# Channels innermost, two additions swapped between VectorE and GpSimd, and new slots, in a kernel of one FFT convolution and one feed-forward block

## The chip, the cores and the metric

One core of a Trainium2 chip. The time is the device time of one execution in microseconds (us). The kernel before took 2484.07 us in the runs that the prediction had (2483.41 to 2486.37). TensorE is PE below, its weight loads PEld, VectorE DVE, ScalarE ACT, GpSimd POOL, SyncE SP. SBUF and PSUM are the two memories in which this kernel keeps its tiles; PE's products are written to tiles in PSUM. All runs in this document are in the fast state and gave correct results. Wherever two kernels are compared, a ratio is the mean time of one kernel's fast runs over that of the other's of the same rounds, on the same chip, so it is not quite the ratio of the medians that stand beside it; the interval after it is the 95% one. Differences of ratios are turned into time with 2481 us, about what the kernel before takes on the chips used.

## The reference

```python
# batch, seq, d = 4, 12544, 128;  d_ff = 768
h = (np.maximum(pos_emb @ w1, 0) @ w2) * np.exp(-0.01 * pos)[:, None]
u = x * v
L = 2 * S
y = irfft(rfft(u, L, axis=1) * rfft(h, L, axis=0)[None], L, axis=1)[:, :S]
a = (x * y).reshape(B * S, D)
hid = maximum(maximum(a @ w1, a @ w2), a @ w3)
out = hid @ w_out
```

Four batches, each a long convolution (by Fourier transforms written as products with tables), then a feed-forward block.

## The kernel before: the parts that matter

The span has four stages: a **prologue** (spectrum of the filter, first half of batch 0); a **loop** of 45 rounds, which makes the rest of batch 0's convolution with nothing beside it; its short **drain**; and the **feed-forward part**, in which PE runs through the blocks of one batch while the convolution of the next is dealt out into "slots", one slot after each `up` (the products pa and pb with their maximum hid, some 3.3 us). An instruction that waits holds up those that stand behind it on its engine: in the profile before, at 793.60 us, ACT begins a turn after 5.93 us of waiting for dt, the hid behind it follows at 794.24, and PE, which had waited 1.90 us for that hid, goes on at 794.79; 28 of PE's 30 waits for ACT's hid before pb end after such a turn.

The first halves land in PSUM and are combined into `spec` in SBUF, two channels (`s`) at a time. Here the innermost index of the write is `k`, so neighbouring elements lie 1024 bytes apart in `spec`:

```python
    def by_r(ps):
        return ps[:].rearrange("p (s m) -> p s m", m=256)[:, :, 0:2 * N1].rearrange(
            "p s (r k) -> p s r k", r=2)

    def over_w(ps, dst, tmp):
        v = by_r(ps)
        nc.scalar.copy(tmp, v[:, :, 1, :])
        for c, op in enumerate((ALU.add, ALU.subtract)):
            nc.vector.tensor_tensor(out=dst[:, :, c, :].rearrange("p k s -> p s k"), in0=tmp,
                                    in1=v[:, :, 0, :], op=op)
```

A group `g` (45 to a batch) is two frequencies: product with the spectrum (`second`, `swap`, `re`, `im`, `sum`), inverse product (`third`), and the sums over halves (`over_c`, `turn`, `pair`, `store`):

```python
    def g_im(g):        # xs *= ht : both inputs in SBUF
        nc.vector.tensor_tensor(out=xss[g][:], in0=xss[g][:], in1=hts.pop(g)[:, 1], op=ALU.mult)

    def g_sum(g):       # xt += xs : both inputs in SBUF ("pointwise sum")
        nc.gpsimd.tensor_tensor(out=xts[g][:], in0=xts[g][:], in1=xss.pop(g)[:], op=ALU.add)
    # ... g_third: PE product, ACT copies half of it out ...
    # g_over_c: dt = c0 +- c1 (DVE, one buffer);  g_turn: two copies of dt on ACT (turn by -i)
    def g_pair(g):      # zs = dt[0:2] +- dt[2:4] : both inputs in SBUF ("sums of k1")
        dt = zss[g]
        zs = state["cv"][0].tile([P, 2, 2, D], FP32, tag="z", name="zs", bufs=2)
        for a, op in enumerate((ALU.add, ALU.subtract)):
            nc.vector.tensor_tensor(out=zs[:, a], in0=dt[:, 0:2, :], in1=dt[:, 2:4, :], op=op)
        zss[g] = zs

    def g_store(b, g):
        nc.gpsimd.dma_start(zd[b][2 * g:2 * g + 2].rearrange("k c t f -> (c t) k f"), ...)
```

The slots in the feed-forward part (the second figure orders the steps within a slot), and the loop:

```python
        s0 = int((NU - done) * 0.6 * per_pair) + 13
        for g in range(NK):
            s = s0 + int(g * per_pair)
            # ... loads
            at(s, 1, g_second, g)
            at(s + 1, 0, g_swap, g)
            at(s + 1, 0, g_re, g)
            at(s + 2, 0, g_im, g)
            at(s + 3, 0, g_sum, g)
            at(s + 5, 1, g_third, g)
            at(s + 6, 0, g_over_c, g)
            at(s + 6, 1, g_turn, g)
            at(s + 7, 1, g_pair, g)
            at(s + 9, 0, g_store, b, g)
    # ...
    for s in range(-1, NK + 5):          # the loop
        # ... s_filter(s), g_second(s), g_swap(s), g_re(s)
        # ... g_turn(s - 3), g_third(s - 2), g_im(s), g_sum(s)
        if 0 <= s - 3 < NK:
            g_pair(s - 3)
        if 0 <= s - 2 < NK:
            g_over_c(s - 2)
        if 0 <= s - 4 < NK:
            g_store(0, s - 4)
```

On DVE and GpSimd there also stand, in every slot, work of the feed-forward block: DVE takes the maximum `hid` (its input pb from PSUM), GpSimd sums of `hid` tiles (SBUF to SBUF). Where a DVE instruction is called blocked below, this is meant: in the profile before, the product xs, both inputs in SBUF, takes 675 to 687 ns in the 106 cases without a two-input instruction of GpSimd beside it, and 1183 ns on average, at most 2315, in the 74 with one; hid, with its input pb from PSUM, takes 559 ns without and 561 with.

Of the kernel before, what the change touches and what calls it, by code (L numbers as in the profile page):

```python
# [9 lines left out]
FP32 = mybir.dt.float32  # L10
I32 = mybir.dt.int32
U16 = mybir.dt.uint16
ALU = mybir.AluOpType
ACTF = mybir.ActivationFunctionType
PSUM = bass.MemoryType.PSUM
P = 128
# [11 lines left out]
N1 = 90  # L28
# [47 lines left out]
def kernel(  # L76
# [15 lines left out]
    nc = tc.nc  # L92
# [5 lines left out]
    NK = N1 // 2  # L98
# [35 lines left out]
    def first_halves(ps, lhs, table):  # L134


        for i, a in enumerate(lhs):
            for r in range(2):
                for c in range(2):
                    nc.tensor.matmul(  # L140
                        ps[64 * c:64 * c + 64, 256 * i + r * N1:256 * i + (r + 1) * N1],
                        a[:, r, :], table[:, r, c * N1:(c + 1) * N1],
                        start=(i % 2 == 0 and r == 0), stop=True, skip_group_check=True)

    def by_r(ps):
        return ps[:].rearrange("p (s m) -> p s m", m=256)[:, :, 0:2 * N1].rearrange(
            "p s (r k) -> p s r k", r=2)

    def over_w(ps, dst, tmp):

        v = by_r(ps)
        nc.scalar.copy(tmp, v[:, :, 1, :])  # L152
        for c, op in enumerate((ALU.add, ALU.subtract)):
            nc.vector.tensor_tensor(out=dst[:, :, c, :].rearrange("p k s -> p s k"), in0=tmp,  # L154
                                    in1=v[:, :, 0, :], op=op)

    def as_it_is(ps, dst):
        nc.scalar.copy(dst.rearrange("p k r s -> p s r k"), by_r(ps))

    def pair_mm(ps, w, x):  # L160

# [72 lines left out]
    sml = fin.enter_context(tc.tile_pool(name="sml", bufs=1))  # L234
# [81 lines left out]
    NU = NG  # L316
# [4 lines left out]
    us, uts, ws, hts, xts, xss, pss, zss = ({} for _ in range(8))  # L321
# [63 lines left out]
    def u_first(u, h):  # L385
        t = uts[u] if h == 0 else uts.pop(u)
        ps = cps.tile([P, 512], FP32, tag="cv", name="ps1")
        at = 4 * u + 2 * h
        first_halves(ps, [t[:, at % 8 + j] for j in range(2)], f1[:])
        tmp = cvp.tile([P, 2, N1], FP32, tag="tmp", name="tmp", bufs=2)  # L390
        over_w(ps, spec[:, :, :, at:at + 2], tmp[:])

    def w_load(g, a):
# [14 lines left out]
    def g_second(g):  # L408
        pss[g] = state["cv"][1].tile([P, 512], FP32, tag="cv", name="ps2")
        pair_mm(pss[g], ws.pop((g, 0)), spec[:, 2 * g:2 * g + 2])  # L410
# [17 lines left out]
        nc.vector.tensor_tensor(out=xss[g][:], in0=xss[g][:], in1=hts.pop(g)[:, 1], op=ALU.mult)  # L428

    def g_sum(g):  # L430
        nc.gpsimd.tensor_tensor(out=xts[g][:], in0=xts[g][:], in1=xss.pop(g)[:], op=ALU.add)  # L431

    def g_third(g):
        ps = state["cv"][1].tile([P, 512], FP32, tag="cv", name="ps3")
# [16 lines left out]
    def g_turn(g):  # L451

        dt = zss[g]
        nc.scalar.copy(dt[0:64, 3, :], dt[64:128, 4, :])  # L454
        nc.scalar.mul(dt[64:128, 3, :], dt[0:64, 4, :], -1.0)  # L455

    def g_pair(g):

        dt = zss[g]
        zs = state["cv"][0].tile([P, 2, 2, D], FP32, tag="z", name="zs", bufs=2)  # L460
        for a, op in enumerate((ALU.add, ALU.subtract)):
            nc.vector.tensor_tensor(out=zs[:, a], in0=dt[:, 0:2, :], in1=dt[:, 2:4, :], op=op)  # L462
        zss[g] = zs

    def g_store(b, g):
        nc.gpsimd.dma_start(
            zd[b][2 * g:2 * g + 2].rearrange("k c t f -> (c t) k f"),
            zss.pop(g)[:].rearrange("p a w d -> p a (w d)"))

    def conv_steps(b, done):  # L470


        out = []

        def at(slot, late, fn, *args):
            out.append((slot, late, len(out), fn, args))



        per_pair = 166 / (NK + 0.6 * (NU - done))  # L480
        for u in range(done, NU):
            s = (u - done) * 0.6 * per_pair + 12
            at(max(0, int(s) - 10), 0, u_load, b, u)
            at(int(s) - 6, 0, u_mul, u)
            at(int(s) - 5, 0, u_planes, u)
            at(int(s) - 4, 0, u_dma, u)
            at(int(s), 0, u_join, u)
            for h in range(2):
                at(int(s + 2 + 0.3 * per_pair * h), 1, u_first, u, h)
        s0 = int((NU - done) * 0.6 * per_pair) + 13  # L490
        for g in range(NK):
            s = s0 + int(g * per_pair)
            at(s - 5, 0, w_load, g, 0)
            at(s - 4, 0, h_load, g)
            at(s, 0, w_load, g, 1)
            at(s, 1, g_second, g)
            at(s + 1, 0, g_swap, g)
            at(s + 1, 0, g_re, g)
            at(s + 2, 0, g_im, g)
            at(s + 3, 0, g_sum, g)  # L500
            at(s + 5, 1, g_third, g)
            at(s + 6, 0, g_over_c, g)
            at(s + 6, 1, g_turn, g)
            at(s + 7, 1, g_pair, g)
            at(s + 9, 0, g_store, b, g)
        slots = {}
        for s, _, _, fn, args in sorted(out, key=lambda r: r[:3]):
            slots.setdefault(s, []).append((fn, args))
        return slots
# [178 lines left out]
    def quad(lhs, table, dst, how):  # L688
        ps = fps.tile([P, 1024], FP32, tag="cv", name="ps1")
        first_halves(ps, lhs, table)  # L690
        if how is as_it_is:
            as_it_is(ps, dst)
        else:
            tmp = sml.tile([P, 4, N1], FP32, tag="tmp", name="tmp", bufs=2)
            how(ps, dst, tmp[:])

    def filter_over_w(k, n):
# [25 lines left out]
    for f in range(0, FO, 4):  # L723
        quad([hs[:, f + i] for i in range(4)], f1h[:], specH[:, :, :, f:f + 4],
             as_it_is)
        u, k = divmod(f // 4, 4)
# [10 lines left out]
    for u in range(0, NU, 2):  # L737
        t = uts.pop(u)
        for v in range(2):
            if u + 4 < NU:  # L740
                u_mul(u + 4 + v, nc.gpsimd if v else nc.vector)
            at = 4 * (u + v)
# [13 lines left out]
    for i in (1, 2):  # L756
        nc.vector.tensor_tensor(out=w_sb[i][:], in0=w_sb[i][:], in1=w_sb[0][:],
                                op=ALU.subtract)
# [3 lines left out]
    cvp = pro.enter_context(tc.tile_pool(name="cvp0", bufs=3))  # L762
# [14 lines left out]
    def s_second(g):  # L777

        ps = gps.tile([P, 512], FP32, tag="g", name="gps")
        for k in range(2):  # L780
            for c in range(2):
                nc.tensor.matmul(ps[64 * c:64 * c + 64, k * P:(k + 1) * P],
                                 specH[:, 2 * g + k, c, :], wf[g][:, k, c, :],
                                 start=(k == 0), stop=True, skip_group_check=True)
        G = cvp.tile([P, 2, 2, 64], FP32, tag="G", name="G", bufs=2)
        nc.scalar.copy(G[:].rearrange("p k c j -> p (k c j)"), ps[:, 0:2 * P])
        Gs[g] = G

    def s_filter(g):


        G = Gs.pop(g)
        ps = sps.tile([P, 1024], FP32, tag="h", name="sps")
        for ri in range(2):
            for k in range(2):
                for c in range(2):
                    for h in range(2):
                        at = 512 * c + (2 * ri + k) * D
                        nc.tensor.matmul(
                            ps[64 * h:64 * h + 64, at:at + D],  # L800
                            G[64 * c:64 * c + 64, k, ri, :], w2x[64 * c:64 * c + 64],
                            start=(ri == 0 and k == 0), stop=True, skip_group_check=True)
        ht = cvp.tile([P, 2, 2, 2, D], FP32, tag="ht", name="ht", bufs=2)
        nc.scalar.copy(ht[:].rearrange("p r k c d -> p (r k) c d"),
                       ps[:].rearrange("p (c m d) -> p m c d", c=2, d=D))
        for c in range(2):
            nc.gpsimd.dma_start(hd[g, 64 * c:64 * c + 64],
                                ht[64 * c:64 * c + 64, c].rearrange("p k q d -> p (k q d)"))
        hts[g] = ht
# [5 lines left out]
    for s in range(-1, NK + 5):  # L815
        if s + 1 < NK:
            s_second(s + 1)
        if 0 <= s < NK:
            s_filter(s)
            ws[s, 0] = wf[s]  # L820
            g_second(s)
            wf.pop(s)
            g_swap(s)
            g_re(s)
        if 0 <= s - 3 < NK:
            g_turn(s - 3)
        if 0 <= s - 2 < NK:
            ws[s - 2, 1] = wi.pop(s - 2)
            g_third(s - 2)
            if s < NK:  # L830
                wi[s] = load_dir(s, 1)
        if 0 <= s < NK:
            g_im(s)
            g_sum(s)
            if s + 4 < NK:
                wf[s + 4] = load_dir(s + 4, 0)
        if 0 <= s - 3 < NK:
            g_pair(s - 3)
        if 0 <= s - 2 < NK:
            g_over_c(s - 2)  # L840
        if 0 <= s - 4 < NK:
            g_store(0, s - 4)

        if s in muls:
            u_mul(muls[s])
        if s in turns:
            u_turn(turns[s])
            u_turn(turns[s] + 1)
        if s in loads:
            u_load(1, loads[s])  # L850
        if NK <= s < NK + 2:
            for v in range(4):
                u_first(2 * (s - NK) + v // 2, v % 2)
# [19 lines left out]
    cvp = ctx.enter_context(tc.tile_pool(name="cvp", bufs=3))  # L873
# [105 lines left out]
```

## Time and profile before

| kernel before | value | read as |
|---|---|---|
| median, four runs | 2484.22 us | the rounds shared with the changed kernel |
| span, PE clock | 2483.5 us, 0.983 | the profiled run |
| PE busy | 2343.1 us (94%) | 140.4 us idle |
| start of round 0, start of the last | 152.14, 354.51 us | first filter product of each round: 202.37 us of loop |
| per round, rounds 4 to 44 | 4.74 us | from the same starts |
| first feed-forward product | 393.29 us | 38.78 us after the last round's start |
| from there to the end | 2090.2 us | the feed-forward part |

The starts are read from the timeline. The lines of the views stand in the prediction. One more view belongs to them: the timeline of one round of the loop. Columns: start, length, engine, line, operation, tiles, in brackets the idle time before and what ended it.

```profile
249.38 0.73 POOL L466 DMA_DIRECT2D zd<-zs  x1
249.78 0.76 DVE L462 TENSOR_TENSOR zs<-dt 128x256 f32<-128x256 f32 x2 [1.79 <-DMA zd<-zs]
250.64 0.76 DVE L447 TENSOR_TENSOR dt<-ps,c 128x256 f32<-128x256 f32 x2
251.45 1.09 PE L131 MATMUL ps<-spec,wt 128*64 128x128 f32 x16 [1.17 <-DVE dt L447]
```

DVE stands 1.79 us until an earlier store has landed and freed a buffer of zs; dt comes after zs on DVE, and PE stands 1.17 us for dt.

### The profile page before, as it was taken

Reading aid. Unit: us, or ns where it says so; the run is one execution under the profiler, and the core shown is the slowest. Engines: PE = TensorE matmul, PEld = TensorE weight load, DVE = VectorE, ACT = ScalarE, POOL = GpSimd, SP = SyncE. Lnnn points to the kernel's source line nnn. Section 1 sums busy time; section 2 is a strip of 40 time slices with the busy share of each in tenths; the row PEclk is TensorE's granted clock in tenths of the full one; section 3 lists DMA queues with packets and bytes.
Section 4 is the critical chain, followed back from the end, with each engine's and each line's share of the span. In section 5 each row is a group of like instructions: output and inputs, shape, how many; then the busy total and the mean of one; then the engine's idle time right before and its main releaser. Section 6 shows DMA issues by size and latency. Waiting matters only on the chain.

```text
span 2483.5 us, 73306 instructions
## 1 busy us (share of the span) xinstructions
PE 2343.1 (94%) x29745; PEld 1651.9 (67%) x29745; DVE 1571.6 (63%) x2981; ACT 1091.4 (44%) x2340; POOL 1532.1 (62%) x1743
## 2 busy tenths in 40 slices
PE   8797778999999999999999999999999999999998
PEld 8686665766666666776666666776666666666665
DVE  5876664766767765766777675766777673333333
ACT  2467763544444433654444443554444442222222
POOL 2766653656676666755666576756676675555465
PEclk8899989999999999999999999999999999999999
DMA  6547766977777747997877757987887753222221
GB/s 152 152 144 234 244 188 148 179 167 206 207 197 207 208 122 154 191 180 200 218 212 210 205 139 168 186 172 206 218 216 210 200 140 82 51 70 58 57 70 21
DMA packets 455227, 408.98 MB, mean 165 GB/s; under 512 B 327132, under 2 KB 331375, under 8 KB 454889
## 3 DMA queue, kind: packets, MB, share of 16 engines
q1 hardware_dynamic: 422240, 315.25, 52.6%
q0 software_dynamic: 32064, 87.60, 11.9%
q8 instruction: 234, 3.83, 0.7%
q10 hardware_dynamic: 585, 1.45, 0.3%
q14 instruction: 104, 0.85, 0.1%
HBM read 295.87 MB, written 84.67 MB: 153 GB/s over the span
## 4 chain that ended last, share of the span: by engine, by line
PE 73%; DVE 7%; ACT 4%; DMA 4%; issue 3%; POOL 1%; SPq 0%; DVEq 0%; ACTq 0%; POOLq 0%
PE ops L608 19%; PE pb L131 19%; PE pa L131 18%; PE ps L131 8%; PE ps L140 4%; PE yps L131 4%; DVE zs L462 3%; DMA zd<-zs 3%; DVE dt L447 2%; ACT hid L559 1%; DVE xs L428 1%; ACT dt L455 1%; DVE hid L562 1%; ACT dt L454 1%; DMA ht<-hd 0%
## 5 line engine op out<-in xcount | busy, mean ns | idle before, releaser
L562 DVE TENSOR_TENSOR hid<-hid,pb 128x392 f32<-128x392 f32 x768 | 429.3, 560 | 481.3 <-PE pb L131 368.6
L131 PE MATMUL pb<-gt,w_sb 128*64 128x392 f32 x3072 | 640.9, 495 | 32.3 <-ACT hid L559 32.0
L131 PE MATMUL pa<-gt,w_sb 128*64 128x392 f32 x3072 | 640.6, 494 | 10.9 <-DVE hid L562 10.9
L559 ACT ACTIVATE hid<-pa 128x392 f32<-128x392 f32 x768 | 380.5, 498 | 590.2 <-PE pa L131 563.3
L131 PEld LDWEIGHTS pb<-gt,w_sb 128*64 128x64 f32 x3072 | 218.6, 137 | 328.0 <-issue 248.0
L630 POOL DMA_DIRECT2D out_dram<-o x256 | 162.4, 639 | 292.2 <-ACT hid L559 140.0
L431 POOL TENSOR_TENSOR xt<-xt,xs 128x512 f32<-128x512 f32 x180 | 234.3, 1302 | 175.2 <-DVE xs L428 94.1
L608 PE MATMUL ops<-hid,wo_sb 128*64 128x196 f32 x3072 | 331.7, 330 | 1.4 <-DVE hid L562 1.4
L462 DVE TENSOR_TENSOR zs<-dt 128x256 f32<-128x256 f32 x360 | 291.2, 849 | 52.4 <-DMA zd<-zs 42.8
L608 PEld LDWEIGHTS ops<-hid,wo_sb 128*64 128x64 f32 x3072 | 222.4, 137 | 138.1 <-issue 116.0
L578 POOL TENSOR_TENSOR s<-hid 128x392 f32<-128x392 f32 x192 | 201.5, 1049 | 146.3 <-DVE hid L562 116.9
L578 POOL TENSOR_TENSOR s<-hid,s 128x392 f32<-128x392 f32 x192 | 201.1, 1048 | 94.2 <-DVE hid L562 91.0
L154 DVE TENSOR_TENSOR spec<-tmp,ps 128x180 f32<-128x180 f32 (+1 forms) x448 | 190.3, 521 | 73.9 <-ACT tmp L152 73.0
L131 PE MATMUL ps<-spec,wt 128*64 128x128 f32 x2880 | 194.4, 278 | 36.8 <-DVE dt L447 33.8
L578 POOL TENSOR_TENSOR hid<-hid,s 128x392 f32<-128x392 f32 x192 | 199.1, 1042 | 42.7 <-DVE hid L562 23.6
L131 PEld LDWEIGHTS pa<-gt,w_sb 128*64 128x64 f32 x3072 | 199.2, 137 | 34.6 <-DVE hid L562 11.0
L140 PE MATMUL ps<-f,uT 98*64 98x90 f32 x4096 | 196.3, 248 | 9.9 <-DVE dt L447 4.5
L578 POOL TENSOR_TENSOR hid<-hid 128x392 f32<-128x392 f32 x192 | 201.0, 1063 | 0.5
L549 DVE TENSOR_TENSOR gt<-yps,xT 128x392 f32<-128x392 f32 x128 | 72.3, 565 | 200.5 <-PE ops L608 147.0
L131 PE MATMUL ps<-xt,wt 128*64 128x128 f32 x2880 | 193.4, 277 | 4.9 <-DVE dt L447 2.7
L140 PEld LDWEIGHTS ps<-f,uT 98*64 98x64 f32 x4096 | 184.0, 142 | 21.0 <-issue 8.1
L131 PEld LDWEIGHTS ps<-spec,wt 128*64 128x64 f32 x2880 | 164.7, 139 | 49.3 <-DVE dt L447 41.2
(101 smaller groups left out, 3200.4 us busy)
## 6 DMA issues: line engine op xcount, KB each, us to landing
wt<-wt_const SPq DMA_DIRECT2D x360, 256.0 KB, 5.0
ht<-hd SPq DMA_DIRECT2D x270, 256.0 KB, 4.5
zd<-zs POOLq DMA_DIRECT2D x180, 256.0 KB, 4.2
zt<-zd SPq DMA_DIRECT2D x256, 180.0 KB, 4.0
ut<-in_xr_dram SPq DMA_DIRECT2D x128, 196.0 KB, 3.6
ut<-in_vr_dram SPq DMA_DIRECT2D x128, 196.0 KB, 3.8
xT<-in_x_dram SPq DMA_DIRECT2D x512, 49.0 KB, 2.9
out_dram<-o POOLq DMA_DIRECT2D x256, 98.0 KB, 3.6
```

What stands on the lines that cost most here:

```text
L131: nc.tensor.matmul(out[64 * h:64 * h + 64], lhsT[:, 64 * h:64 * h + 64], rhs, start=start, stop=stop, skip_group_check=True)
L140: nc.tensor.matmul(ps[64 * c:64 * c + 64, 256 * i + r * N1:256 * i + (r + 1) * N1], a[:, r, :], table[:, r, c * N1:(c + 1) * N1], start=(i ...
L154: nc.vector.tensor_tensor(out=dst[:, :, c, :].rearrange("p k s -> p s k"), in0=tmp, in1=v[:, :, 0, :], op=op)
L431: nc.gpsimd.tensor_tensor(out=xts[g][:], in0=xts[g][:], in1=xss.pop(g)[:], op=ALU.add)
L447: nc.vector.tensor_tensor(out=dt[:, w:w + 4:2 + w, :] if w == 0 else dt[:, 1:5:3, :], in0=c0, in1=c1[:], op=op)
L462: nc.vector.tensor_tensor(out=zs[:, a], in0=dt[:, 0:2, :], in1=dt[:, 2:4, :], op=op)
L549: nc.vector.tensor_tensor(out=g[:].rearrange("d (w t) (m a) -> d w t m a", w=2, a=2), in0=y, in1=xT.rearrange("d w t (m a) -> d w t m a", ...
L559: nc.scalar.activation(h[:], pa[:, 0:N], Relu)
L562: nc.vector.tensor_tensor(out=h[:], in0=h[:], in1=pb[:, 0:N], op=ALU.max)
L578: nc.gpsimd.tensor_tensor(out=out[:], in0=a[:], in1=b[:], op=op)
L608: nc.tensor.matmul(ps[64 * c:64 * c + 64, 0:H2], w, rhs[:, H2 * c:H2 * c + H2], start=start, stop=True, skip_group_check=True)
L630: nc.gpsimd.dma_start(dst[64 * m:64 * m + 64, 64 * c + 2 * i:64 * c + 2 * i + 4, b, :], t[m][64 * c:64 * c + 64].rearrange("d k (q n) -> d ...
```

## The change

The intent: writes to `spec` in pairs of neighbours; a fairer split of the SBUF-to-SBUF additions between DVE and GpSimd; ACT not standing in front of dt; the loop's store issued as soon as its sums are there. The chain of a group's second half (`third` to `store`) stays in its old absolute slots except that `turn` and `pair` come later, because `s0` goes up by one while `third`, `over_c` and `store` go down by one relative to it. The first half is compressed: `im` and `sum` now share a slot.

```diff
     def by_r(ps):
         return ps[:].rearrange("p (s m) -> p s m", m=256)[:, :, 0:2 * N1].rearrange(
-            "p s (r k) -> p s r k", r=2)
+            "p s (r k) -> p r k s", r=2)
     def over_w(ps, dst, tmp):
         v = by_r(ps)
-        nc.scalar.copy(tmp, v[:, :, 1, :])
+        nc.scalar.copy(tmp, v[:, 1])
         for c, op in enumerate((ALU.add, ALU.subtract)):
-            nc.vector.tensor_tensor(out=dst[:, :, c, :].rearrange("p k s -> p s k"), in0=tmp,
-                                    in1=v[:, :, 0, :], op=op)
+            nc.vector.tensor_tensor(out=dst[:, :, c, :], in0=tmp, in1=v[:, 0], op=op)
     # ... as_it_is and both tmp tiles likewise: [.., N1, 2] and [.., N1, 4]
     def g_sum(g):
-        nc.gpsimd.tensor_tensor(out=xts[g][:], ...)
+        nc.vector.tensor_tensor(out=xts[g][:], ...)
     def g_pair(g):
-            nc.vector.tensor_tensor(out=zs[:, a], ...)
+            nc.gpsimd.tensor_tensor(out=zs[:, a], ...)
-        s0 = int((NU - done) * 0.6 * per_pair) + 13
+        s0 = int((NU - done) * 0.6 * per_pair) + 14
             at(s + 2, 0, g_im, g)
-            at(s + 3, 0, g_sum, g)
-            at(s + 5, 1, g_third, g)
-            at(s + 6, 0, g_over_c, g)
-            at(s + 6, 1, g_turn, g)
-            at(s + 7, 1, g_pair, g)
-            at(s + 9, 0, g_store, b, g)
+            at(s + 2, 0, g_sum, g)
+            at(s + 4, 1, g_third, g)
+            at(s + 5, 0, g_over_c, g)
+            at(s + 6, 0, g_turn, g)
+            at(s + 7, 0, g_pair, g)
+            at(s + 8, 0, g_store, b, g)
     # the loop
             g_pair(s - 3)
+            g_store(0, s - 3)
             ...
-        if 0 <= s - 4 < NK:
-            g_store(0, s - 4)
```

More of the change, by code (lines that the diff above doesn't have):

```diff
@@ L146, in by_r @@
         return ps[:].rearrange("p (s m) -> p s m", m=256)[:, :, 0:2 * N1].rearrange(
-            "p s (r k) -> p s r k", r=2)
+            "p s (r k) -> p r k s", r=2)
     def over_w(ps, dst, tmp):
         v = by_r(ps)
-        nc.scalar.copy(tmp, v[:, :, 1, :])
+        nc.scalar.copy(tmp, v[:, 1])
         for c, op in enumerate((ALU.add, ALU.subtract)):
-            nc.vector.tensor_tensor(out=dst[:, :, c, :].rearrange("p k s -> p s k"), in0=tmp,
-                                    in1=v[:, :, 0, :], op=op)
+            nc.vector.tensor_tensor(out=dst[:, :, c, :], in0=tmp, in1=v[:, 0], op=op)
     def as_it_is(ps, dst):
-        nc.scalar.copy(dst.rearrange("p k r s -> p s r k"), by_r(ps))
+        nc.scalar.copy(dst.rearrange("p k r s -> p r k s"), by_r(ps))
     def pair_mm(ps, w, x):
@@ L389, in u_first @@
         first_halves(ps, [t[:, at % 8 + j] for j in range(2)], f1[:])
-        tmp = cvp.tile([P, 2, N1], FP32, tag="tmp", name="tmp", bufs=2)
+        tmp = cvp.tile([P, N1, 2], FP32, tag="tmp", name="tmp", bufs=2)
         over_w(ps, spec[:, :, :, at:at + 2], tmp[:])
@@ L430, in g_sum @@
     def g_sum(g):
-        nc.gpsimd.tensor_tensor(out=xts[g][:], in0=xts[g][:], in1=xss.pop(g)[:], op=ALU.add)
+        nc.vector.tensor_tensor(out=xts[g][:], in0=xts[g][:], in1=xss.pop(g)[:], op=ALU.add)
     def g_third(g):
@@ L461, in g_pair @@
         for a, op in enumerate((ALU.add, ALU.subtract)):
-            nc.vector.tensor_tensor(out=zs[:, a], in0=dt[:, 0:2, :], in1=dt[:, 2:4, :], op=op)
+            nc.gpsimd.tensor_tensor(out=zs[:, a], in0=dt[:, 0:2, :], in1=dt[:, 2:4, :], op=op)
         zss[g] = zs
@@ L693, in quad @@
         else:
-            tmp = sml.tile([P, 4, N1], FP32, tag="tmp", name="tmp", bufs=2)
+            tmp = sml.tile([P, N1, 4], FP32, tag="tmp", name="tmp", bufs=2)
             how(ps, dst, tmp[:])
```

## The prediction

> **What bounds the kernel now.** I began with the busy shares: TensorE (PE) 2343.1 of 2483.5 us, VectorE (DVE) 1571.6, GpSimd (POOL) 1532.1, ScalarE (ACT) 1091.4. PE is busy 94%, so at most 140.4 us of its idle time can be won, unless its clock rises. I then cut the span by stages.
>
> ```profile
> core 0: us, PE busy (x) PEld busy (x) DVE busy (x) ACT busy (x) POOL busy (x), PEclk, DMA share, GB/s
> 70.00:130.00 60.00, 45.25 (x742) 41.41 (x740) 57.92 (x87) 20.38 (x31) 51.40 (x46) 0.86 0.54 130
> 164.00:364.00 200.00, 155.38 (x3006) 135.60 (x3002) 135.03 (x259) 141.94 (x296) 128.84 (x169) 0.95 0.73 229
> 364.00:392.00 28.00, 18.45 (x270) 15.58 (x272) 14.89 (x43) 8.90 (x29) 2.75 (x4) 0.79 0.34 98
> 560.00:910.00 350.00, 332.12 (x3866) 228.27 (x3864) 241.30 (x435) 153.50 (x347) 226.47 (x237) 0.99 0.72 199
> 910.00:1120.00 210.00, 207.40 (x2686) 141.65 (x2684) 136.90 (x291) 104.64 (x225) 134.76 (x174) 1.00 0.82 162
> 1120.00:1470.00 350.00, 335.31 (x4004) 234.16 (x4002) 257.29 (x451) 158.29 (x359) 231.28 (x241) 1.00 0.77 206
> 1690.00:2025.00 335.00, 323.41 (x3837) 228.20 (x3832) 247.66 (x436) 152.37 (x346) 225.94 (x235) 0.99 0.77 208
> ```
>
> PE idles 14.8 us in the prologue's 70 to 130, where DVE is 97% busy and is the bound; 44.6 us in the first loop (164 to 364, batch 0's spectra with nothing beside them); 9.6 us in its drain; and 17.9 + 14.7 + 11.6 = 44.2 us in the three stretches of the feed-forward part that carry the second half of a later batch's convolution. Elsewhere it is nearly full (2.6 us idle in 910 to 1120). The waits name the causes; the first line and the store line are of the loop, the next two of 560 to 2025.
>
> ```profile
> PE ps L131 <- DVE dt L447: 36.5, 28, 3.9
> ...
>   DVE zs L462: 42.8, 26
> ...
> PE pb L131 <- ACT hid L559: 30.8, 28, 1.9
> PE pa L131 <- DVE hid L562: 9.9, 11, 1.6
> ...
> ACT dt L454 <- DVE dt L447: 277.3, 159, 5.9
> ```
>
> In the loop PE waits for DVE's dt, and DVE waits 42.8 us for the stores of zs to release one of its two buffers. In the feed-forward part PE waits mostly for ACT, which has stood in front of the turn by -i (L454) until DVE made dt: 277.3 us over the run.
>
> **Durations.** From the groups, one shape per line; names and shapes, count, busy us, mean ns.
>
> ```profile
> L562 DVE TENSOR_TENSOR hid<-hid,pb 128x392 f32<-128x392 f32 x768 | 429.3, 560 | 481.3 <-PE pb L131 368.6 <-ACT hid L559 101.3 <-PE ops L608 9.3
> L462 DVE TENSOR_TENSOR zs<-dt 128x256 f32<-128x256 f32 x360 | 291.2, 849 | 52.4 <-DMA zd<-zs 42.8 <-ACT xs L417 4.7 <-ACT ht L804 3.5
> L428 DVE TENSOR_TENSOR xs<-xs,ht 128x512 f32<-128x512 f32 x180 | 159.9, 889 | 0.0
> L154 DVE TENSOR_TENSOR spec<-tmp,ps 128x180 f32<-128x180 f32 x384 | 145.6, 476 | 66.0 <-ACT tmp L152 65.3
> L447 DVE TENSOR_TENSOR dt<-ps,c 128x256 f32<-128x256 f32 x360 | 134.8, 415 | 4.8 <-ACT c L438 0.3
> L549 DVE TENSOR_TENSOR gt<-yps,xT 128x392 f32<-128x392 f32 x128 | 72.3, 565 | 200.5 <-PE ops L608 147.0 <-PE yps L131 31.1 <-DMA wt<-wt_const 9.1
> L154 DVE TENSOR_TENSOR spec<-tmp,ps 128x360 f32<-128x360 f32 x64 | 44.7, 793 | 7.9 <-ACT tmp L152 7.7
> ```
>
> zs and dt have one size, but zs takes twice as long: its two inputs are both in SBUF, dt's are not. spec with 180 elements takes longer than dt with 256: it writes single elements 1024 bytes apart.
>
> [...] zs has a minimum of 410 ns and a mean of 849, xs a minimum of 675 and a mean of 889. [...] for DVE's reads the trace shows no cost: gt reads PSUM 196 bytes apart and takes 565 ns, contiguous hid 560. [...] here the 512-element sum takes 1302 ns against 684 for DVE's 512-element product from PSUM.
>
> **The change, part by part.**
>
> *Channels innermost.* PSUM is now read with steps, SBUF written in pairs (fours in the prologue). dt has 415 ns for 256 elements, hid 560 for 392: 1.07 ns an element. So 180 elements should take about 415 - 76 x 1.07 = 334 ns, 360 about 526. Busy time hides overlap: dt's is 374 each, spec's now 379 and 698. Taking off the same 41 ns, I get 293 and 485, so DVE is spared 384 x 86 ns = 33 us and 64 x 213 ns = 13.6 us. The first lies mostly beside a full PE. Of the second, 40 of 64 instructions are in the stretch that DVE bounds (8.5 us), some in its neighbours; GpSimd there is 86% busy and caps the gain. ScalarE's 16 four-channel copies should fall from 1508 to about 800 ns, but PE is full beside them. Prologue: -10 us.
>
> *Sums of k1 on GpSimd, pointwise sum on DVE.* Off DVE: 360 zs, 291 us. On it: 180 sums of 512, 0.69 unblocked, some 1.0 blocked, 180 us. With channels innermost DVE goes to about 1571.6 - 291 + 180 - 47 = 1414 us. Off GpSimd: 180 x 1.30 = 234 us; on it: 360 of 256. Its own rows are 1042 at 392 and 1302 at 512, 2.17 ns an element, so about 750 ns, 270 us: 1568 us, or 63%, no bound.
>
> *The first loop.* In the order of time round 4's filter product starts at 165.09 and round 44's at 354.51: 4.73 us a round over 40. PE needs 1.10 + 1.09 + 1.04 + 0.61 = 3.84. Over two rounds a buffer of zs passes through: zs 0.76 to 1.83, dt 0.76, xt 0.6, xs 0.7, GpSimd's sum 1.27, store issued and landed 4.2, that is 8.3 to 9.4, or 4.1 to 4.7 a round. It is this ring, not the engines, that sets the round. Afterwards the store follows its sums in the same round and has most of two rounds to land: the ring is cut. A new one forms: turn 0.61, zs on GpSimd 1.5, dt 0.76, with 0.3 of semaphores and up to 0.7 blocked by DVE's sum: 3.2 to 3.9. ACT needs 3.6, GpSimd 1.08 + 1.5 + 0.73 = 3.3. So I take 4.15 with the turns of the next batch and DMA jams in it (a round moves 1 MB; 247 GB/s, against 296 at most now): 40 x 0.58 = 23 us, of which I keep 21. The drain wins 1.
>
> *Turn a slot later.* dt is now made at slot +5 and turned at +6; before, both stood in +6. A slot is about 3.3 us, so ACT should mostly find dt ready. Of the 40.7 us that PE waits for hid in 560 to 2025, I take 60% off: -24 us.
>
> Sum: -10 - 21 - 1 - 24 = -56, 2428. I keep 2 us back for the added collisions.
>
> **Rivals.** (1) *GpSimd in dt's way.* dt has a single buffer, so DVE's next dt waits until GpSimd has read the last. Rounds lie 2.6 slots apart, so in two of five the next dt shares the slot of the sums on GpSimd, which is also 65% busy there and stands up to 6.9 us in front of out_dram. If DVE stalls, hid comes late: for it speaks the strict order; against it, that zs stalls of 2.7 to 3.8 us now cost PE only 9.9 us. It would leave half of the 24: 2442. (2) *DMA or ACT takes over the loop.* DMA is already at 0.73, ACT at 3.6 of 3.84 a round. Then a round stays at 4.5 and the loop gives 9: 2442. (3) *Strided PSUM reads cost*, 0.7 ns an element as the writes did: the prologue gives nothing, 2440. All three: about 2460. (4) On the other side, the clock is granted lower where PE idles (0.86 and 0.95 above); filled gaps could shorten matmuls too, and PE may lose all 40 us of its waits: 2412.
>
> **Range and chances.** Each of the three large terms may miss by half, mostly independently: some 12 us either way. Range 2412 to 2452. The limit of 2% lies at 2434.4, a little above my number: faster by over 2% 0.6, within 2% 0.39, slower 0.01.
>
> **What would show it.** spec at 330 to 360 and 520 to 560 ns; the sum at 0.7 to 1.1 us on DVE; zs near 750 ns on GpSimd; no wait of zs for its store in the loop, which ends near 340 from a start near 155; ACT's wait for dt under 120 us; PE idle in the three stretches under 25 us together. It is wrong if DVE's dt waits long for GpSimd's zs, if the spec rows don't fall, or if the loop's rounds stay over 4.4 us.

## The result

The changed kernel took 2429.36 us (median of four, 2425.31 to 2432.93) beside 2484.22 us (2483.41 to 2486.37) for the kernel before: ratio 0.9777 (0.976 to 0.9795), faster by over 2%. The prediction was 2430. Its total was right; the way there was not right in every step, and the stages show it first. All times are from the two profiled runs (spans 2483.5 and 2426.1 us, 57.4 apart; the medians above are 54.9 apart).

| stage | before, us | after, us | gained | predicted |
|---|---|---|---|---|
| prologue (start of round 0) | 152.14 | 140.85 | 11.3 | 10 |
| loop (round 0 to the last round's start) | 202.37 | 174.85 | 27.5 | 21 |
| drain (to the first feed-forward product) | 38.78 | 38.16 | 0.6 | 1 |
| feed-forward part | 2090.2 | 2072.2 | 18.0 | 24 |

PE's busy time fell too, from 2343.1 to 2325.7 us at the same 29745 instructions, its clock rose from 0.983 to 0.989, and its idle time fell from 140.4 to 100.4 us. So 40.0 us of the gain are filled gaps and 17.4 us are shorter matmuls.

The stretches of the changed kernel that answer to those in the prediction (same columns: stretch, us, busy us of PE, PEld, DVE, ACT, POOL with counts, PE clock, DMA share, GB/s). The first is the prologue's, the second the whole loop, the last three the stretches of the feed-forward part that carry the second half of a later batch, some 39 to 58 us earlier than before:

```profile
70.00:130.00 60.00, 50.73 (x940) 46.40 (x937) 55.66 (x103) 25.14 (x39) 57.25 (x51) 0.94 0.66 156
140.85:315.70 174.85, 153.68 (x3144) 133.57 (x3145) 147.35 (x214) 146.99 (x301) 144.81 (x205) 0.99 0.85 262
521.00:871.00 350.00, 337.71 (x3981) 233.28 (x3978) 247.63 (x407) 157.93 (x356) 246.24 (x292) 1.00 0.73 199
1074.00:1424.00 350.00, 338.31 (x4006) 234.57 (x4004) 250.17 (x415) 159.72 (x359) 243.76 (x286) 1.00 0.75 204
1636.00:1967.00 331.00, 321.29 (x3816) 223.44 (x3814) 236.52 (x394) 152.54 (x343) 234.04 (x275) 0.99 0.78 210
```

In the prologue's stretch PE does 5.5 us more work; in the loop the clock is 0.99. In the last three stretches PE is still idle for 12.3 + 11.7 + 9.7 = 33.7 us, where it was 44.2. GpSimd, at 70%, is now as busy as DVE there.

What waited for whom in the changed kernel, whole run (engine and tile that waited, what it waited for; total us, times, longest):

```profile
ACT dt L453 <- DVE dt L446: 73.7, 69, 2.9
...
DVE dt L446 <- POOL zs L461: 34.1, 42, 2.2
...
PE ops L607 <- DVE hid L561: 16.3, 8, 3.5
PE ps L131 <- DVE dt L446: 12.8, 25, 2.6
...
PE ps L131 <- DVE xt L430: 10.6, 15, 1.2
```

ACT's wait for dt fell from 277.3 to 73.7 us, PE's wait for dt from 36.5 in the loop alone to 12.8 in all, and the 30.8 us that PE waited for ACT's hid in the feed-forward part are down to 1.2 us in the row of its products. Two lines are new or much longer: before its products ops PE waits 16.3 us for DVE's hid (1.4 before), and it waits 10.6 us for the pointwise sum xt. Its older wait for DVE's hid, 10.9 us before pa, is gone. So most of the wait on ACT was traded for one on DVE.

The groups of the changed kernel that were swapped or re-laid (count, then busy us, mean ns, idle before):

```profile
L461 POOL TENSOR_TENSOR zs<-dt 128x256 f32<-128x256 f32 x360 | 282.6, 806 | 26.8 <-ACT dt L454 24.6 <-DVE xt L422 1.1 <-ACT c L437 0.2
L430 DVE TENSOR_TENSOR xt<-xt,xs 128x512 f32<-128x512 f32 x180 | 236.7, 1315 | 6.2
L427 DVE TENSOR_TENSOR xs<-xs,ht 128x512 f32<-128x512 f32 x180 | 189.6, 1054 | 0.0
L154 DVE TENSOR_TENSOR spec<-tmp,ps 128x180 f32<-128x180 f32 x384 | 112.3, 337 | 73.7 <-ACT tmp L152 72.8
L154 DVE TENSOR_TENSOR spec<-tmp,ps 128x360 f32<-128x360 f32 x64 | 30.7, 521 | 11.0 <-ACT tmp L152 11.0
```

spec fell to 337 and 521 ns. But the sum takes 1315 ns on DVE, more than the 1302 it took on GpSimd, and xs, which nobody touched, rose from 889 to 1054: both read two tiles from SBUF. Without a two-input instruction of GpSimd beside them the sum and xs take 692 and 682 ns on average (63 and 50 cases), with one 1651 and 1196 (117 and 130). A timeline further down shows GpSimd holding up one such sum. The wait of zs for its store is gone from its row.

The timeline of a round of the loop in the changed kernel, to be laid beside the one above:

```profile
193.01 1.83 POOL L461 TENSOR_TENSOR zs<-dt 128x256 f32<-128x256 f32 x2
194.88 0.76 DVE L446 TENSOR_TENSOR dt<-ps,c 128x256 f32<-128x256 f32 x2 [1.30 <-POOL zs L461]
195.14 0.73 POOL L465 DMA_DIRECT2D zd<-zs  x1 [0.30 <-POOL zs L461]
195.69 1.09 PE L131 MATMUL ps<-spec,wt 128*64 128x128 f32 x16
```

The store follows its own sums within 0.3 us. DVE's dt now waits 1.30 us for GpSimd to have read the last dt, and PE's product after it starts without a wait.

### The profile page after: what moved, and what is told of

The parts are those of the page before. It is cut to its first block, busy times and chain, and to the rows that moved or that the text cites. A ratio compares the mean times of both kernels' runs of the same rounds, so it can differ in the third digit from the quotient of the medians.

```text
span 2426.1 us, 72839 instructions
## 1 busy us (share of the span) xinstructions
PE 2325.7 (96%) x29745; PEld 1630.8 (67%) x29745; DVE 1514.7 (62%) x2801; ACT 1086.8 (45%) x2340; POOL 1586.1 (65%) x1923
## 3 DMA queue, kind: packets, MB, share of 16 engines
q1 hardware_dynamic: 422240, 315.25, 54.9%
## 4 chain that ended last, share of the span: by engine, by line
PE 77%; POOL 8%; DVE 6%; DMA 4%; issue 4%; ACT 1%; SPq 1%; ACTq 0%; POOLq 0%; DVEq 0%
PE ops L607 19%; PE pa L131 19%; PE pb L131 19%; PE ps L131 8%; PE ps L140 6%; PE yps L131 4%; POOL zs L461 3%; DVE xs L427 1%; DVE xt L430 1%; DMA zt<-zd 1%; POOL zd L465 1%; DVE dt L446 1%; POOL hd L806 1%; PE pm L301 1%; DMA wt<-wt_const 1%
## 5 line engine op out<-in xcount | busy, mean ns | idle before, releaser
L607 PE MATMUL ops<-hid,wo_sb 128*64 128x196 f32 x3072 | 331.9, 329 | 16.3 <-DVE hid L561 16.3
L461 POOL TENSOR_TENSOR zs<-dt 128x256 f32<-128x256 f32 x360 | 282.6, 806 | 26.8 <-ACT dt L454 24.6
L430 DVE TENSOR_TENSOR xt<-xt,xs 128x512 f32<-128x512 f32 x180 | 236.7, 1315 | 6.2
L577 POOL TENSOR_TENSOR hid<-hid,s 128x392 f32<-128x392 f32 x192 | 205.7, 1074 | 48.4 <-DVE hid L561 28.3
L131 PE MATMUL ps<-xt,wt 128*64 128x128 f32 x2880 | 191.8, 276 | 15.7 <-DVE xt L430 10.6
L140 PE MATMUL ps<-f,uT 98*64 98x90 f32 x4096 | 192.2, 245 | 9.2 <-DVE dt L446 4.2
L154 DVE TENSOR_TENSOR spec<-tmp,ps 128x180 f32<-128x180 f32 (+1 forms) x448 | 143.0, 363 | 84.8 <-ACT tmp L152 83.9
L427 DVE TENSOR_TENSOR xs<-xs,ht 128x512 f32<-128x512 f32 x180 | 189.6, 1054 | 0.0
```

Source lines behind the costliest of these rows:

```text
L131: nc.tensor.matmul(out[64 * h:64 * h + 64], lhsT[:, 64 * h:64 * h + 64], rhs, start=start, stop=stop, skip_group_check=True)
L140: nc.tensor.matmul(ps[64 * c:64 * c + 64, 256 * i + r * N1:256 * i + (r + 1) * N1], a[:, r, :], table[:, r, c * N1:(c + 1) * N1], start=(i ...
L154: nc.vector.tensor_tensor(out=dst[:, :, c, :], in0=tmp, in1=v[:, 0], op=op)
L430: nc.vector.tensor_tensor(out=xts[g][:], in0=xts[g][:], in1=xss.pop(g)[:], op=ALU.add)
L461: nc.gpsimd.tensor_tensor(out=zs[:, a], in0=dt[:, 0:2, :], in1=dt[:, 2:4, :], op=op)
L577: nc.gpsimd.tensor_tensor(out=out[:], in0=a[:], in1=b[:], op=op)
```

## The experiments

Theories at the outset. **T** (the prediction's): the ring through the two buffers of zs (sums, store, landing, and only then a free buffer for the next sums) set the loop's round and the earlier store cuts it; the layout shortens the prologue; the later turn relieves ACT in the feed-forward part. **Rivals**: the loop was relieved by the swap of engines, not by the store; the feed-forward part's gain is the swap's, or something in it costs and hides part of a larger gain. The one rival that could not be tried is that dt's single buffer now holds DVE up: with a second buffer for dt the kernel did not build, so no run shows it.

### The parts alone

`e1_layout_alone` is the kernel before with the layout hunks of the diff and nothing else.

> The kernel before with channels innermost alone. If the layout is worth what DVE bounds in the prologue and nothing beside a full PE: the first filter product starts 10 to 11 us earlier (141 to 142 us), the loop's 4.73 us a round and the feed-forward part are unchanged, 2471 to 2476 us. Rival: the 33 us freed on DVE later also shorten PE's waits for hid; then 2455 to 2465 us.

Measured: 2465.54 us beside 2479.33, ratio 0.9946 (0.9931 to 0.9961), some 13 us. Round 0 starts at 140.50 us, 11.6 earlier than in the profile before; a round takes 4.63 us. The layout is the prologue's gain, nearly alone. (The time lies under the expected 2471 to 2476 us, but in these rounds the kernel before is itself 4.9 us faster than in those that the range was worked from.)

`e2_store_at_once_alone` is the kernel before with the loop's store moved:

```diff
             g_pair(s - 3)
+            g_store(0, s - 3)
         if 0 <= s - 2 < NK:
             g_over_c(s - 2)
-        if 0 <= s - 4 < NK:
-            g_store(0, s - 4)
```

> The kernel before with the loop's store moved into the round of its sums, engines and slots as before. If the ring through the two zs buffers set the round, cutting it alone gives 4.1 to 4.3 us a round and 2464 to 2470 us, and DVE's wait of 42.8 us for the stores falls below 5 us. Rival: DVE, blocked by GpSimd, set the round and the store only filled the time; then the round stays above 4.5 us and the time above 2476 us.

Measured: 2448.73 us, 0.9873 (0.9857 to 0.989), some 31 us, and 4.13 us a round. The loop went from 202.37 to 177.81 us (150.21 to 328.02), 24.6 us, and DVE's wait for the stores fell to 0.7 us (160 to 320 us). So the store alone cuts the ring, with the sums still on DVE: the swap is not needed for it (the changed kernel has 4.08). The total is 7 us more than the loop's gain. The profile's feed-forward part is 8 us shorter too (2081.9), but on another chip, whose kernel before is 5 us faster; about 3 us stay unexplained. The total is also well under the expected 2464 to 2470 us.

### The ring in the loop

`e3_loop_store_late` is the changed kernel with the loop's store put back to where it was.

```diff
             g_pair(s - 3)
-            g_store(0, s - 3)
         if 0 <= s - 2 < NK:
             g_over_c(s - 2)
+        if 0 <= s - 4 < NK:
+            g_store(0, s - 4)
```

> The changed kernel with the loop's store put back one round later. On GpSimd the store then stands behind the next sums, which wait for the store before it: if the ring is the cause, a round takes a store's 4.2 us and the sums' 1.5 us and 0.3 us of semaphores, 6.0 us, so 65 to 80 us more than the changed kernel: 2495 to 2510 us. Rival: the engine swap freed the loop by itself; then within 10 us of the changed kernel, under 2440 us.

Measured: 2473.5 us, 0.9975 (0.996 to 0.999); 5.14 us a round, more than before. The bracket is the wait for a store to land:

```profile
244.35 1.40 POOL L461 TENSOR_TENSOR zs<-dt 128x256 f32<-128x256 f32 x2 [3.00 <-DMA zd<-zs]
245.70 0.73 POOL L465 DMA_DIRECT2D zd<-zs  x1
```

With zs and the store both on GpSimd, each sum waits for the store just issued: the landing (3.3 us in the median here) and the sums, 1.4, make 4.7 of the 5.14. I had expected 6.0 with a landing of 4.2 us, taken from the kernel before; the mechanism held, the landing was mis-sized. It also shows that in the changed kernel the early store is worth 0.9975 - 0.9777 = 0.0198, 49 us, much more than the 31 it is worth alone. Without it the swap makes the loop worse: 5.14 us a round here, 4.63 in e1, which has the late store and the new layout too, but the old engines.

`e7_late_three_zs` gives e3 a third buffer of zs in the loop (two small tiles there, tmp and w1t, go down to one to make room).

```diff
-        zs = state["cv"][0].tile([P, 2, 2, D], FP32, tag="z", name="zs", bufs=2)
+        zs = state["cv"][0].tile([P, 2, 2, D], FP32, tag="z", name="zs", bufs=state["zb"])
-    state = {"cv": (cvp, cps), "turn": cps, "xb": 2, "xsb": 2}
+    state = {"cv": (cvp, cps), "turn": cps, "tb": 1, "xb": 2, "xsb": 2, "zb": 3}
```

> The changed kernel with the loop's store a round later, as in e3, but with a third zs buffer in the loop (room made by single tmp and w1t buffers there, which only the drain feels). If e3's loss is the ring through two buffers, the third buffer undoes it: 4.1 to 4.2 us a round against e3's 5.14, GpSimd's wait for the stores under 5 us, ratio 0.977 to 0.982. Rival: the late store's place on GpSimd's queue is what costs; then the round stays near 5.1 us and the ratio near 0.997.

Measured: 2434.06 us beside 2479.51, 0.9808 (0.9791 to 0.9824); 4.10 us a round. In the loop zs waited 63.7 us for its stores in e3; here, by the same view:

```profile
POOL zs L461 <- DMA zd<-zs: 0.8, 1, 0.8
```

The late store does next to no harm once there is a third buffer: 4.10 us a round against 4.08 in the changed kernel, and 0.9808 against 0.9777 and, in a repeat below, 0.9785, with intervals that overlap. So it is the ring through the two buffers, and nothing else about the store's place that these runs can tell apart.

### Engines and slots in the feed-forward part

From here on all kernels have the new layout and the loop's early store, and differ in two things: which engine does the pointwise sum and the sums of k1, and the slots. Three sets of slots: the old ones, the change's, and a third (e8's), which keeps the first half as it was and moves only `turn` and `pair` later.

`e4_old_slots`: the changed kernel with the old slots.

```diff
-        s0 = int((NU - done) * 0.6 * per_pair) + 14
+        s0 = int((NU - done) * 0.6 * per_pair) + 13
-            at(s + 2, 0, g_sum, g)  ... third s+4, over_c s+5, turn s+6, pair s+7, store s+8
+            at(s + 3, 0, g_sum, g)  ... third s+5, over_c s+6, turn s+6 (late), pair s+7 (late), store s+9
```

> The changed kernel with the old slots of the feed-forward part (pointwise sum at 3, third at 5, dt and turn both in 6, sums at 7 late, store at 9). If the later turn freed ACT: ACT's wait for dt goes back above 180 us, PE's wait for hid by ACT above 15 us, 2438 to 2446 us; loop and prologue as in the changed kernel. Rival: the swap of engines did it and the slots matter little: 2427 to 2433 us.

Measured: 2418.44 us, 0.9749 (0.9735 to 0.9764). This is faster than both the expectation (2438 to 2446 us) and its rival (2427 to 2433). The change with its old slots is faster than with its new ones: the intervals of e4 and of the change overlap slightly (0.9764 above 0.976), but on one chip, in the same rounds, the feed-forward part takes 2059.8 us in e4 and 2071.3 in e3, which has the change's slots. This is so although ACT's wait for dt is back at 192.2 us and PE's for ACT's hid at 24.8. So, with the new engines, the new slots cost more than they give.

`e6_old_slots_old_engines`: e4 with the sums on GpSimd and the sums of k1 on DVE again, that is, the kernel before with layout and early store.

```diff
     def g_sum(g):
-        nc.vector.tensor_tensor(
+        nc.gpsimd.tensor_tensor(
     def g_pair(g):
-            nc.gpsimd.tensor_tensor(
+            nc.vector.tensor_tensor(
```

> The kernel before with channels innermost and the loop's store at once, nothing else. If the two add up, 0.9946 x 0.9873 = 0.982 of the kernel before. Against the run with old slots and new engines (0.975) it shows what the swap alone is worth at the old slots: 0.007, some 17 us, if they add; near zero if the swap only matters together with the new slots.

Measured: 2436.4 us beside 2481.66, 0.9819 (0.9802 to 0.9836): just the sum of e1 and e2 (0.0054 + 0.0127 = 0.0181). Nothing shows that those two parts depend on each other.

`e5_old_engines`: the change's slots, old engines (the same edit as in e6, applied to the changed kernel).

> The changed kernel with the old engines (pointwise sum on GpSimd, sums of k1 on VectorE), new slots and everything else kept. If the swap is worth its place because zs on DVE is blocked by GpSimd: zs on DVE back to 850 ns or more in the feed-forward part, 5 to 15 us slower than the changed kernel. Rival: with the new slots the swap costs, since the sum on DVE stands blocked 1.3 us behind xs and PE waits 10.6 us for it; then 3 to 10 us faster. The loop's ring is cut in both: 4.0 to 4.2 us a round.

Measured: 2412.91 us, 0.9724 (0.9708 to 0.9739), and `a0_after_again`, the changed kernel unedited in the same call:

> The changed kernel itself, for comparison on the same chip as the three that follow: a ratio of 0.977 to 0.979 to the kernel before.

Measured: 2428.85 us, 0.9785 (0.9765 to 0.9804), as the first time. In the change's slots the swap of engines costs 0.0061, 15 us; in the old slots (e6 to e4, from two calls) it gains 0.0070, 17 us. For e5 the rival in the expectation came true, and by more than it said.

`e8_sum_and_turn_late`: the changed kernel, but the first half keeps its old slots.

```diff
-        s0 = int((NU - done) * 0.6 * per_pair) + 14
+        s0 = int((NU - done) * 0.6 * per_pair) + 13
-            at(s + 2, 0, g_sum, g)
-            at(s + 4, 1, g_third, g)
-            at(s + 5, 0, g_over_c, g)
-            at(s + 6, 0, g_turn, g)
-            at(s + 7, 0, g_pair, g)
-            at(s + 8, 0, g_store, b, g)
+            at(s + 3, 0, g_sum, g)
+            at(s + 5, 1, g_third, g)
+            at(s + 6, 0, g_over_c, g)
+            at(s + 7, 0, g_turn, g)
+            at(s + 8, 0, g_pair, g)
+            at(s + 9, 0, g_store, b, g)
```

> New engines; pointwise sum in slot 3 and third in 5 as in the old slots, dt in 6, but turn in 7 and sums in 8, so the turn is a slot later as the change meant it and the sum is not pulled forward. If what went wrong with the new slots is the sum pulled next to xs on DVE: ACT's wait for dt falls below 100 us as in the changed kernel, PE's wait for the sum below 3 us, and it beats the old slots: 0.970 to 0.974. Rival: turning later itself costs, because dt's single buffer is held longer; then it is as slow as the changed kernel, 0.977 to 0.979.

Measured: 2393.89 us (2392.10 to 2394.91), 0.9646 (0.963 to 0.9662): the fastest of all. It beats both kernels, and the expected 0.970 to 0.974. From the pointwise sum on, every step stands in the same slot, counted from the start, as in the change; only loads, spectrum product, swap and the two products come a slot earlier. That alone is worth 0.9785 - 0.9646 = 0.0139, 34 us. And from e4 to e8 only turn and pair move: 0.0103, 26 us, nearly the 24 that the prediction gave to that move. The waits of e8 in its feed-forward part, 521 to 1960 us, answer to those of the changed kernel above:

```profile
ACT dt L453 <- DVE dt L446: 61.5, 47, 2.2
...
PE ops L607 <- DVE hid L561: 2.6, 4, 0.9
...
PE ps L131 <- DVE xt L430: 0.4, 1, 0.4
```

ACT's wait is low as in the change, and the two new waits of PE are nearly gone (in the repeat of the change they are 16.3 and 9.6 us in the same window). PE is busy 1427.2 of these 1439 us, in the repeat of the change 1402.4.

What happens in the change's slots shows best where a sum is stuck; a stretch of the changed kernel's timeline:

```profile
658.46 1.04 DVE L427 TENSOR_TENSOR xs<-xs,ht 128x512 f32<-128x512 f32 x1
...
658.89 1.49 POOL L577 TENSOR_TENSOR hid<-hid,s 128x392 f32<-128x392 f32 x1
...
659.54 3.74 DVE L430 TENSOR_TENSOR xt<-xt,xs 128x512 f32<-128x512 f32 x1
...
660.35 1.40 POOL L461 TENSOR_TENSOR zs<-dt 128x256 f32<-128x256 f32 x2
...
661.73 1.00 POOL L577 TENSOR_TENSOR hid<-hid,s 128x392 f32<-128x392 f32 x1
...
663.33 1.09 PE L131 MATMUL ps<-xt,wt 128*64 128x128 f32 x16 [0.91 <-DVE xt L430]
```

DVE's product xs and the sum xt come one right after the other. The sum starts at 659.54, while GpSimd is in a sum; GpSimd goes on with two zs and another sum, back to back, until 662.73, and DVE's sum ends at 663.28. PE, which needs the sum for its next product, has stood idle for 0.91 us by then. From the sum to PE's product there are as many slots in e8 as here. But in e8 xs, the product that the sum needs, stands a slot earlier, so that the sum has not to start behind it, and a delay of xs has a slot to pass in before the sum needs it.

Is it DVE's total time in these instructions? The groups of e8 in the same part say no:

```profile
L427 DVE TENSOR_TENSOR xs<-xs,ht 128x512 f32<-128x512 f32 x133 | 194.7, 1464 | 0.0
L430 DVE TENSOR_TENSOR xt<-xt,xs 128x512 f32<-128x512 f32 x133 | 150.6, 1132 | 0.0
```

In the repeat of the change the means are 1043 and 1318 ns. Together they are longer in e8 (2596 against 2361 ns), so DVE stands in them for longer, and the kernel is faster. The total of these delays is not what decides; where they fall is the remaining reading, which the next run tests.

`e11_im_a_slot_earlier` tests this with one figure of the changed kernel:

```diff
-            at(s + 2, 0, g_im, g)
+            at(s + 1, 0, g_im, g)
             at(s + 2, 0, g_sum, g)
```

> The changed kernel with one number changed: the product xs a slot earlier (1 for 2), so that xs and the pointwise sum no longer stand in one slot on DVE. From the loads to the sums the rest keeps the changed kernel's slots. If these two SBUF-SBUF operations back to back are what PE waits for: PE's waits for the sum and for hid fall from 26 us to under 6 us, ratio 0.964 to 0.970. Rival: it was the lateness of the whole first half (the spectrum product, swap and first product also stand a slot later than in e8): 0.976 to 0.980.

Measured: 2398.47 us beside 2479.51, 0.9666 (0.9649 to 0.9683): 0.0119 better than the repeat of the change, 29 of the 34 us. In the same window as above PE's two waits are down to this:

```profile
PE ops L607 <- DVE hid L561: 1.2, 2, 0.7
...
PE ps L131 <- DVE xt L430: 0.3, 1, 0.3
```

One figure undoes nearly all of it: the product and the sum in one slot were most of the cost. The other steps of the first half are left where the change put them; what they cost is at most the small rest, and the intervals of e11 and e8 overlap.

`e10_late_turn_old_engines` is e8 with the old engines (the edit of e6).

> The slots of e8 (sum 3, third 5, dt 6, turn 7, sums of k1 8) with the old engines. If the swap of engines earns its place once the slots suit it: 0.970 to 0.976 against 0.9646 of e8. Rival: with good slots the engines do not matter, or GpSimd is better left alone: 0.961 to 0.966.

Measured: 2400.1 us, 0.9672 (0.9646 to 0.9698). In e8's slots the swap is worth 0.0026, with overlapping intervals: unsettled. With the old engines the later turn is worth more, from e6 to e10 0.0147 or 36 us, so engines and slots do not simply add.

The compression costs something with the old engines too: from e10 to e5, in both of which the sum is GpSimd's, 0.0052 or 13 us (from two calls; the intervals do not overlap). In e5 PE waits for that sum, and in e10 it has no such wait:

```profile
PE ps L131 <- POOL xt L430: 16.4, 17, 2.1
```

So the squeezed schedule, with the sum right after its product, is harmful by itself; the sum on DVE makes it dearer. How much of the 34 us is the squeeze and how much the blocking of DVE by GpSimd is not separated further.

`e9_all_on_dve` is e8 with the sums of k1 of the feed-forward part back on DVE, so that both stand there.

```diff
-    def g_pair(g):
+    def g_pair(g, eng=nc.vector):
-            nc.gpsimd.tensor_tensor(out=zs[:, a], ...)
+            eng.tensor_tensor(out=zs[:, a], ...)
-            g_pair(s - 3)
+            g_pair(s - 3, nc.gpsimd)      # in the loop, as it was
```

> The slots of e8 with a third placing in the feed-forward part: the pointwise sum and the sums of k1 both on DVE, GpSimd with neither (the loop keeps the sums on GpSimd). If, with slots that leave each result a slot to be late, the engine hardly matters: 0.963 to 0.969, like e8 (0.9646) and e10 (0.9672). Rival: four SBUF-SBUF operations a group on DVE, each blocked by GpSimd's sums, make hid late: above 0.972.

Measured: 2441.86 us beside 2479.72, 0.9845 (0.9831 to 0.9858), 49 us slower than e8. PE waits 20.0 us for DVE's hid and 14.3 for the sum. The rival in the expectation came true. So the placement is not indifferent: in these slots it pays to leave one of the two on GpSimd; which one makes no difference that these runs can settle (e8 and e10).

All kernels of this part in one table, ratios to the kernel before:

| slots | sum on GpSimd, k1 on DVE | sum on DVE, k1 on GpSimd | both on DVE |
|---|---|---|---|
| old | 0.9819 (e6) | 0.9749 (e4) | |
| the change's | 0.9724 (e5) | 0.9785 (a0) | |
| the change's, product a slot earlier | | 0.9666 (e11) | |
| e8's | 0.9672 (e10) | 0.9646 (e8) | 0.9845 (e9) |

## Why the prediction was right, and where it was not

**The total.** 2430 against 2429.36. Partly this is luck, because two errors cancelled: the loop gave 6.5 us more than was taken for it, and the feed-forward part 6.0 us less, by the profiles. The steps one by one:

**Channels innermost: right.** That pairs of neighbours would be enough was the author's estimate; no row of the profile before showed it. The run does: spec measures 337 and 521 ns where 334 and 526 had been worked out, the four-channel copy on ACT 760 ns; the prologue gave 11.3 us, and e1 11.6 by itself.

**The loop: mechanism right, size low.** The ring is confirmed from three sides: e2 cuts it alone, e3 brings it back, e7 undoes it with a buffer. The loop gave 27.5 us instead of 21. The mis-sized terms: the round is 4.08, not 4.15, so that 40 rounds give 26.3 us where 23.2 was worked out (3.1 more); the first four rounds, which the sum left out, give 1.2; and the 2.2 us that were kept back did not get lost. Rival (2) therefore fell: neither DMA (0.85 busy, 262 GB/s) nor ACT (147.0 of 174.85 us) kept the round at 4.5 us. The mark "ends near 340 from a start near 155" is off at both ends (315.70 from 140.85): the start had not been given the prologue's gain, and the length it implied, 185 us, was 174.85.

**The durations after the swap: wrong.** The sum was put at some 1.0 us and measures 1315 ns, and xs was left at 889 and measures 1054. 180 x 315 + 180 x 165 ns = 86 us, which is most of the difference between the 1414 us expected of DVE and the 1514.7 measured. zs is 806 rather than 750 ns; GpSimd's 1586.1 us against 1568 is near. DVE was no bound in total (1514.7 of 2426.1 us), so these misses did not by themselves spoil the number; they announce the next one.

**Turn a slot later: the step that failed.** "Of the 40.7 us that PE waits for hid in 560 to 2025, I take 60% off: -24 us." The move itself gives this: 26 us from e4 to e8, and 36 with the old engines. But the step treated it as the only thing that happens in the feed-forward part. Two terms were missing. The swap of engines gives 17 us in the old slots (e6 to e4). And the compressed first half, which puts two SBUF-to-SBUF instructions of DVE behind each other in one slot, costs 34 us once the sum is on DVE (e8 to a0), and 13 us with the sum on GpSimd (e10 to e5). 17 + 26 - 34 = 9 us is what engines and slots give together, by the ratios 0.9819 - 0.9785 = 0.0034, 8 us. The feed-forward part of the profile gave 18.0; e6's, with layout and early store alone, is already 7 us shorter than before's, on another chip, and how much of that is the chip's is not settled. On that chip it takes 2083.2 us in e6 and 2075.5 in a0: 7.7 us for engines and slots, which agrees. The mark "PE idle in the three stretches under 25 us" failed for this reason, with 33.7; besides the sum's duration, which missed its 0.7 to 1.1 us, it was the only mark that pointed to the missing term.

**Rivals.** (1) GpSimd in dt's way: dt does wait 34.1 us for zs, but PE's wait for dt is small (12.8 us), and e8 with 27.7 us of that wait in its feed-forward part is the fastest. Its own test, a second dt buffer, did not build. Harm came by another instruction than the one named: the sum, which stands blocked behind GpSimd in the timeline above. (3) Reads of PSUM in steps of 1024 bytes show no cost (337 and 521 ns, beside 334 and 526 worked out), as argued. (4) Shorter matmuls: 17.4 us of the 57.4 are PE's busy time, at a higher granted clock; in the loop the clock went from 0.94 to 0.99. That the filled gaps cause it was not tested, and e1 speaks against so simple a link: its clock is 0.990 (0.984 to 0.987 for the kernel before in the same rounds), although PE is still idle for 136.1 us, and in its stretch from 70 to 130 us the clock is 1.00 with PE 80% busy. The cause of the clock stays open. The range on that side, 2412, was not reached by the change, but e8 went past it.

## What to carry to other kernels

When the steps of a pipeline are dealt out to slots, check for each move which other steps it pushes together: here a move that gave 26 us came with a compression that cost 34, and one figure in the schedule got 29 back. Count the waits of the engine that bounds, not the busy or blocked time of the others: in the fastest kernel xs and the sum together take longer (2596 ns against 2361), but a slot lies between the two. And a store that frees a buffer belongs right behind the sums that fill it, where buffers are few: here that gave 31 us by itself (e2), and with a third buffer the late store cost next to nothing (4.10 us a round against 4.08); with the store late, moving the sums to the store's own engine made the ring tighter (5.14 us a round against 4.74).

## What the traces show of DVE beside GpSimd, and of reads of PSUM

- When GpSimd has a row of instructions, the runs show both outcomes for a DVE instruction with two SBUF inputs. The sum at 659.54 us took 3.74 us, through the rest of one GpSimd sum, two zs and another sum, against 0.67 to 0.69 us for the shortest of its kind in these runs: it ended 0.55 us after the last of them. But xs just before it, at 658.46, took 1.04 us: it lay over the end of one GpSimd sum and the start of the next, which took 1.49 us against 1.00 for its like at 661.73. In the trace of the changed kernel 32 of the 180 sums last over two or more whole two-input GpSimd instructions, the other 148 over at most one. So the wait can be that of a whole row, but need not be; what decides it is not known.
- DVE's reads of PSUM with steps of 1024 bytes showed no cost here: 337 ns for 180 elements and 521 for 360, against 334 and 526 worked out from contiguous reads (dt, 415 ns for 256 elements, and hid, 560 for 392).
